# Infini-attention with a gated GLU on one core: warming products, the order of the first norms, the absolute Q in two parts, an engine for the bound rows, and the place of one weight load

## The chip, the cores and the metric

The kernel runs on one core of a Trainium2 chip. The metric is the time of one execution in microseconds. The core has five engines that run their own instruction streams: TensorE (PE in the profile, with its weight loads as PEld), VectorE (DVE), ScalarE (ACT), GpSimd (POOL) and SyncE (SP), which here only issues DMAs. ScalarE also issues a few DMAs. Each stream is executed in its written order.

## What is computed

```python
def _A_ref(x, wq, wk, wv, wo, beta):
...
    phi = lambda t: jnp.where(t > 0, t + 1.0, jnp.exp(t))
    g = _sigmoid(beta).reshape(1, H, 1, 1)
    for s in range(N):
        qs, ks, vs = (q[:, :, s].copy(), k[:, :, s].copy(), v[:, :, s].copy())
        logits = jnp.einsum('bhqd,bhkd->bhqk', qs, ks) * scale + mask
        p = _softmax(logits, axis=-1)
        a_dot = jnp.einsum('bhqk,bhkd->bhqd', p, vs)
        pq = phi(qs)
        num = jnp.einsum('bhld,bhde->bhle', pq, M)
        den = jnp.einsum('bhld,bhd->bhl', pq, z)[..., None] + 1e-06
        a_mem = num / den
        o = g * a_mem + (1.0 - g) * a_dot
        outs.append(o)
        pk = phi(ks)
        M = M + jnp.einsum('bhld,bhle->bhde', pk, vs)
        z = z + jnp.einsum('bhld->bhd', pk)
...
    return o @ wo

def _B_ref(x, w_gate, w_up, w_down):
    g = jnp.einsum('bsd,df->bsf', x, w_gate)
    u = jnp.einsum('bsd,df->bsf', x, w_up)
    h = _sigmoid(g) * u
    return jnp.einsum('bsf,fd->bsd', h, w_down)

x = A_x
xn = _layernorm(x, axis=-1)
s = _A_ref(xn, A_wq, A_wk, A_wv, A_wo, A_beta)
g = _silu(_B_ref(xn, B_w_gate, B_w_up, B_w_down))
return x + s * g
```

In the first function x is the normed input, 2048 x 640; there are 32 heads of 20 and N = 4 segments of L = 512 rows; F is 1536. The result is bfloat16, 2048 x 640.

## The kernel before, in words

The 2048 rows are four segments of 512. A segment's normed input stands transposed in `xnT` (five chunks of 128 channels by 512 rows). From it come K and Q, transposed (`ktd`, `qtd`, five chunks of 128 x 512 each, from `do_K` and `do_Q`), V by rows (`do_V(n, j, half)`: row tile j, 320 columns), and the gate and up products of the GLU (`do_gate`, `do_up`, twelve each a segment).

**Bound.** The softmax subtracts no maximum that is found from the scores. Instead a bound is computed ahead: `do_K` keeps the largest absolute K of each channel (`kabs`), `bound` spreads it over heads (`ik`, line 318) and takes the absolute values of Q (`aq`, line 322, one VectorE instruction over 128 x 2560), and `bound_mm` multiplies the two (five products, line 330) into PSUM tile `cps` of 96 rows. Line 333 copies them to `cb` on VectorE, line 334 writes them to DRAM, and `bound_dma` brings them back as three more rows of each head of `QT`. The tile `aq` shares its one buffer with `odot` (tag `oq`), in which the parts of the memory read-out of a segment are collected and written to DRAM by `mem_spill`.

**Start.** Lines 639 to 703 are written in order by hand. TensorE multiplies zeros (`keep_warm`, 128 x 128 by 128 x 512, into `wps`) until the first tile is there. VectorE makes the statistics of each row tile in two halves (`half_stats0`), ScalarE the root for tiles 0 and 1 (`root0`), GpSimd the power for tiles 2 and 3 (`ln_rstd`), and VectorE the normed tile (`norm0`, line 249). TensorE transposes it, and the transposed tile is copied from PSUM: tile 0 in two parts (`first_transpose`, line 665 on ScalarE, line 663 on VectorE), tiles 1 and 2 on ScalarE (line 266), tile 3 on VectorE (line 268). Between the transposes stand the eight V products. Then follow K and Q of segment 0 (lines 705 to 715), its bound, and the first gate and up products.

**Queue of SP.** After `bound_mm(0)` SP brings back the bound rows of heads 0 to 15, loads the next input (`load_x(1)`, line 141), writes the second part of K and Q (`spill`, line 307), reads K back transposed (`k_tok`, line 374), brings K and Q into the head layout (`relayout`, line 313) with the bound rows of heads 16 to 31, and only then loads `Wd` (line 728, 1920 KB) and `Wo`.

**Body.** From line 734 a planner writes the rest: 20 slots a segment. A slot begins with the scores of one unit (line 541, into the single PSUM tile `Sps`) and their exponential on ScalarE (line 549); between the scores the planner puts dense products and, at the fractions of a slot that `TIMES` lists, the other steps for the next segment m: among them K at 9.75 to 14.4, Q at 11.5 to 13.7, `bound` at 14.8, `bound_mm` at 15.9. A step with a cost of 0 moves no product. All PSUM tiles other than `Sps` come from a pool of four (`ps_d`); a product that needs a new one waits until its last reader is done.

Of the kernel before, what the change touches and what calls it, by code (L numbers as in the profile page):

```python
# [9 lines left out]
P = 128  # L10
# [5 lines left out]
L = 512  # L16
F = 1536
DC = D // P
# [6 lines left out]
BF = mybir.dt.bfloat16  # L25
F32 = mybir.dt.float32
ACT = mybir.ActivationFunctionType
ALU = mybir.AluOpType
# [27 lines left out]
def segment_units(n):  # L56
# [11 lines left out]
    stats0=(0.83, 1.2, 1.95, 3.9), stats=(-0.55, 0.42, 1.32, 3.57), norm=(5.2, 5.75, 6.03, 6.18),  # L68
    norm_T=7.22, ready=12.0, K=(9.75, 10.18, 10.6, 13.9, 14.4), Q=(11.5, 11.9, 12.47, 12.67, 13.7),
    K_eng='vaava', Q_eng='avvav', V=(10.3, 13.3, 14.4, 14.6, 16.35, 17.45, 19.75, 19.85), V_eng='avaavvav',  # L70
    k_spill0=14.77, k_lay0=15.15, q_spill0=14.1, q_lay0=16.33, q_spill1=15.26, k_spill1=17.0, bound=14.8,
    bound_mm=15.9, bound_lay0=18.6, load_x=14.7, phi_k=((7.08, 7.78, 8.23), (12.7, 12.8, 13.7)),
    phi_q=((16.0, 16.6, 17.12), (18.3, 18.7, 19.18)),
)
# [7 lines left out]
def kernel(  # L82
# [14 lines left out]
    nc = tc.nc  # L97
# [160 lines left out]
    def ln_transpose(n, j, xn, eng):  # L258
        if n not in xnT_of:
            xnT_of[n] = xpool.tile([P, DC, L], BF, name="xnT")  # L260
        pT = ps_d.tile([P, DC, P], BF, name="pT", tag="d")
        for c in range(DC):
            nc.tensor.transpose(pT[:, c, :], xn[:, c * P:(c + 1) * P], ident[:])
        dst = xnT_of[n][:, :, j * P:(j + 1) * P]
        if eng is nc.scalar:
            nc.scalar.copy(dst, pT[:])
        else:
            nc.vector.tensor_copy(dst, pT[:])
# [41 lines left out]
    def relayout(n, half, dd, dst, eng):  # L310
        src = dd[n % 2][320 * half:320 * (half + 1), :].rearrange("(g r d) n -> r d g n", g=4, r=4)
        for r in range(4):
            eng.dma_start(dst[32 * r:32 * r + DH, 4 * half:4 * half + 4, :], src[r])

    def bound(n):
        s = seg[n]
        ik = stg.tile([P, DC, H], BF, name="ik")
        nc.vector.tensor_tensor(ik[:], Ind[:].rearrange("p c r g -> p c (r g)"),
                                s["kabs"][:].unsqueeze(2).to_broadcast([P, DC, H]), op=ALU.mult)
        aq = stg.tile([P, DC, L], BF, name="aq", tag="oq")  # L320
        U16 = mybir.dt.uint16
        nc.vector.tensor_scalar(aq[:].bitcast(U16), s["qt"][:].bitcast(U16), 0x7FFF, None, op0=ALU.bitwise_and)
        s["bound"] = ik, aq

    def bound_mm(n):
        ik, aq = seg[n]["bound"]
        cps = ps_d.tile([3 * H, L], F32, name="cps", tag="d")
        for c in range(DC):
            i = c % 3
            nc.tensor.matmul(cps[H * i:H * i + H, :], lhsT=ik[:, c, :], rhs=aq[:, c, :],  # L330
                             start=(c < 3), stop=(c >= 2), tile_position=(0, H * i), skip_group_check=True)
        cb = stg.tile([3 * H, L], BF, name="cb")
        nc.vector.tensor_copy(cb[:], cps[:])  # L333
        nc.sync.dma_start(Bd[n % 2][:], cb[:])

    def bound_dma(n, half):
# [5 lines left out]
    def do_V(n, j, half, evac):  # L342
        ps = ps_d.tile([P, HD], F32, name="psv", tag="d")
        for k in range(DC):
            mm(ps[:], xnT_of[n][:, k, j * P:(j + 1) * P], Wv[:, k, half * HD:(half + 1) * HD],
               k == 0, k == DC - 1)
        dst = V[n % 2][:, j, half * 16:(half + 1) * 16, 0:DH]
        src = ps[:].rearrange("p (h e) -> p h e", e=DH)
        if evac is nc.scalar:
            nc.scalar.copy(dst, src)  # L350
        else:
            nc.vector.tensor_copy(dst, src)
# [282 lines left out]
    def keep_warm(k):  # L635
        for _ in range(k):
            nc.tensor.matmul(wps[:], lhsT=warm[:, 0:P], rhs=warm[:, 0:L], start=True, stop=True)  # L637

    keep_warm(11)
    mv, rs = ln_tiles(0)  # L640
    new_seg(0)
    xns, sts = {}, {}
# [1 line left out]
    def half_stats0(j, i):  # L644
        if i == 0:
            sts[j] = lnp.tile([P, 2, 6], F32, name="st")
        nc.vector.bn_stats(sts[j][:, i, :], xt_of[0][:, j, i * HD:(i + 1) * HD])
        if i == 1:
            nc.vector.bn_aggr(mv[:, j, :], sts[j][:])
# [4 lines left out]
    def first_transpose():  # L654

        xnT_of[0] = xpool.tile([P, DC, L], BF, name="xnT")
        for c0, c1 in ((0, 2), (2, 5)):
            pT = ps_d.tile([P, c1 - c0, P], BF, name="pT", tag="d")
            for c in range(c0, c1):
                nc.tensor.transpose(pT[:, c - c0, :], xns[0][:, c * P:(c + 1) * P], ident[:])  # L660
            dst = xnT_of[0][:, c0:c1, 0:P]
            if c0:
                nc.vector.tensor_copy(dst, pT[:])
            else:
                nc.scalar.copy(dst, pT[:])
# [9 lines left out]
    half_stats0(1, 0)  # L675
    norm0(0)
    half_stats0(1, 1)
    first_transpose()
    root0(1)
    load_w(nc.scalar, Wg, B_w_gate)  # L680
    half_stats0(2, 0)
    norm0(1)
    half_stats0(2, 1)
    ln_rstd(mv, rs, slice(2, 3))
# [1 line left out]
    half_stats0(3, 1)  # L686
    ln_rstd(mv, rs, slice(3, 4))
    norm0(2)
    keep_warm(2)
    do_V(0, 0, 0, nc.scalar)  # L690
    ln_transpose(0, 1, xns[1], nc.scalar)
    norm0(3)
# [3 lines left out]
    do_V(0, 1, 0, nc.scalar)  # L696
    ln_transpose(0, 2, xns[2], nc.scalar)
    do_V(0, 1, 1, nc.scalar)
    do_V(0, 2, 0, nc.scalar)
    ln_transpose(0, 3, xns[3], nc.vector)  # L700
    do_V(0, 2, 1, nc.scalar)
    do_V(0, 3, 0, nc.scalar)
    do_V(0, 3, 1, nc.scalar)
# [4 lines left out]
            spill(0, 0, nc.sync, None)  # L708
    for c in range(3):
        do_Q(0, c, nc.scalar)  # L710
    spill(0, 0, None, nc.sync)
    relayout(0, 0, Kd, KT, nc.sync)
    relayout(0, 0, Qd, QT, nc.sync)
    for c in range(3, 5):
        do_Q(0, c, nc.scalar)
    bound(0)
    finish(do_gate(0, 0))
    finish(do_up(0, 0))
    bound_mm(0)
    bound_dma(0, 0)  # L720
    load_x(1)
    spill(0, 1, nc.sync, nc.sync)
    k_tok(0)
    relayout(0, 1, Kd, KT, nc.sync)
    relayout(0, 1, Qd, QT, nc.sync)
    bound_dma(0, 1)
    gates()
    nc.sync.dma_start(Wd[:], B_w_down.rearrange("(f p) n -> p f n", p=P))
    load_w(nc.sync, Wo, A_wo)
    for f in (1, 2, 3, 4):  # L730
        finish(do_gate(0, f))
# [68 lines left out]
    for n in range(NSEG):  # L800
        t0 = n * SEG

        def on(name, ns, fn, *items):
            times = TIMES[name]
            for i, it in enumerate(items):
                at(t0 + (times[i] if isinstance(times, (list, tuple)) else times), ns, fn, *it)

        if n >= 1:
            on("dot6", 0, dot_spill, (n - 1, 4, 7))
            on("load6", 0, out_load, (n - 1, 0, C4))  # L810
            on("dot7", 0, dot_spill, (n - 1, 7, 8))
            on("load7", 0, out_load, (n - 1, C4, D))
            if n >= 2:
                on("add", 0, out_add, (n - 1, 0, DC - 1), (n - 1, DC - 1, DC))
            on("out", V_NS, out_item, *[(n - 1, i) for i in range(8)])
            on("update", 700, m_update, (n - 1,))
            on("mem", MEM_NS, mem_part, *[(n, i % 4, i // 4) for i in range(8)])
            on("mem_spill", 0, mem_spill, (n,))
            on("mem_T_last" if n == NSEG - 1 else "mem_T", 0, mem_T, (n,))
            if n < NSEG - 1:  # L820
                on("k_tok", 0, k_tok, (n,))
        on("dot3", 0, dot_spill, (n, 0, 4))
        if n == NSEG - 1:
            on("dot5", 0, dot_spill, (n, 4, 6))
            on("load5", 0, out_load, (n, 0, 6 * 4 * DH))
            on("add5", 0, out_add, (n, 0, 3))
            continue
        m = n + 1
        on("stats0" if n == 0 else "stats", 0, stats, *[(m, j) for j in range(4)])
        on("norm", 0, norm, *[(m, j) for j in range(4)])  # L830
        on("norm_T", 0, ln_dmaT, (m,))
        on("ready", 0, ready.add, (m,))
        at(t0 + TIMES["K"][0] - 0.001, 0, new_seg, m)
        on("K", GLU_NS, do_K, *[(m, c, EVAC[TIMES["K_eng"][c]]) for c in range(DC)])
        on("Q", GLU_NS, do_Q, *[(m, c, EVAC[TIMES["Q_eng"][c]]) for c in range(DC)])
        on("V", V_NS, do_V, *[(m, i // 2, i % 2, EVAC[TIMES["V_eng"][i]]) for i in range(8)])
        on("k_spill0", 0, spill, (m, 0, nc.sync, None))
        on("k_lay0", 0, relayout, (m, 0, Kd, KT, nc.sync))
        on("q_spill0", 0, spill, (m, 0, None, nc.sync))
        on("q_lay0", 0, relayout, (m, 0, Qd, QT, nc.sync))  # L840
        on("q_spill1", 0, spill, (m, 1, None, nc.sync))
        on("k_spill1", 0, spill, (m, 1, nc.sync, None))
        on("bound", 0, bound, (m,))
        on("bound_mm", C_NS, bound_mm, (m,))
        on("bound_lay0", 0, bound_dma, (m, 0))
        at(t0 + SEG - 0.003, 0, relayout, m, 1, Kd, KT, nc.sync)
        at(t0 + SEG - 0.002, 0, relayout, m, 1, Qd, QT, nc.sync)
        at(t0 + SEG - 0.001, 0, bound_dma, m, 1)
        for name, sg, key in (("phi_k", n, "ktok"), ("phi_q", m, "qt")):
            for i, (c0, c1) in enumerate(((0, 2), (2, 4 if key == "ktok" else 5))):  # L850
                for fn, t, a in zip((phi_min, phi_exp, phi_end), TIMES[name][i], ((sg, key, c0, c1), (), ())):
                    at(t0 + t, 0, fn, *a)
        if n + 2 < NSEG:
            on("load_x", 0, load_x, (n + 2,))
# [105 lines left out]
```

## Time and profile before

| what | us |
|---|---|
| three runs: median (lowest to highest) | 321.97 (320.97 to 322.71) |
| the profiled execution: its own time | 322.08 |
| the profiled execution: span of its instructions | 320.4 |
| TensorE busy | 310.9 |
| VectorE, ScalarE, GpSimd busy | 230.9, 225.2, 137.4 |
| first warming product, first transpose, first K product begin | 1.24, 5.91, 14.51 |
| first scores begin | 36.83 |
| `bound` of segments 1, 2, 3: `aq` begins | 88.86, 155.84, 222.51 |

All times in the text are from the start of the span. A line of the timeline gives start, duration, engine, line, operation, tiles written and read, and in brackets the idle time before it with what ended it. A product's line reaches past the moment at which the next may start: five products of 320 columns start 0.136 us apart and their group reads 0.84 us.

### The profile page before, as it was taken

What the parts mean: (1) busy time and instruction counts of PE and PEld (TensorE: products, weight loads), DVE (VectorE), ACT (ScalarE), POOL (GpSimd) and SP (SyncE); (2) the same over time, 40 slices, a digit from 0 to 9 for tenths busy, and PEclk for the clock granted to TensorE, in tenths of its full rate; (3) what the DMA queues carried; (4) which work ended last, traced back from release to release, by engine and by line L of the source; (5) the groups of instructions that cost most, each with busy time, mean ns of one, the idle gap of its engine ahead of it and who ended that gap; (6) DMA issues with size and microseconds to landing.
All of it is one profiled execution on the core that took longest, in us unless ns stands there. A gap on an engine that the chain in (4) does not pass through costs nothing.

```text
span 320.4 us, 10046 instructions
## 1 busy us (share of the span) xinstructions
PE 310.9 (97%) x4218; PEld 167.4 (52%) x4247; DVE 230.9 (72%) x503; ACT 225.2 (70%) x225; POOL 137.4 (43%) x231
## 2 busy tenths in 40 slices
PE   8999999999999999999999999999999999999994
PEld 3544434665445445654575445545466645445673
DVE  5384265765779888997778999977877686734555
ACT  3623478788798777777897868778797766776730
POOL 1780035525273445334553364444533353435324
PEclk9999999999999999999999999999999999999999
DMA  7974679320742362606683383436544000350302
GB/s 258 366 308 145 175 165 355 101 49 2 212 149 67 106 156 84 124 23 195 192 188 94 108 127 100 104 119 197 121 133 125 18 23 23 117 133 3 98 19 82
DMA packets 56086, 41.36 MB, mean 129 GB/s; under 512 B 26953, under 2 KB 54665, under 8 KB 56041
## 3 DMA queue, kind: packets, MB, share of 16 engines
q1 hardware_dynamic: 53496, 35.97, 40.5%
q10 hardware_dynamic: 2544, 4.75, 4.0%
q8 instruction: 33, 0.54, 0.7%
q14 instruction: 13, 0.10, 0.1%
HBM read 19.90 MB, written 14.78 MB: 108 GB/s over the span
## 4 chain that ended last, share of the span: by engine, by line
PE 93%; DVE 2%; ACT 2%; issue 1%; POOL 1%; DVEq 0%; ACTq 0%
PE yp L130 11%; PE up L130 11%; PE gp L130 10%; PE psq L130 9%; PE Sps L541 8%; PE gp L134 6%; PE up L134 5%; PE yp L134 5%; PE ApsT L565 5%; PE psv L130 4%; PE psq L134 4%; PE sp L130 3%; PE sp L134 3%; PE sp L527 2%; PE wps L637 2%
## 5 line engine op out<-in xcount | busy, mean ns | idle before, releaser
L549 ACT ACTIVATE pt<-Sps 128x2048 bf16<-128x2048 f32 (+1 forms) x81 | 150.3, 1856 | 42.4 <-PE Sps L541 38.8
L551 POOL TENSOR_SCALAR_AFFINE_SELECT pt<-pt 128x512 bf16<-128x512 bf16 x128 | 82.7, 661 | 158.5 <-ACT pt L549 158.4
L433 DVE SCALAR_TENSOR_TENSOR hT<-tg,up 128x512 bf16<-128x512 bf16 x48 | 32.3, 674 | 22.9 <-PE up L130 8.4
L130 PE MATMUL up<-xnT,Wu 128*128 128x512 bf16 x147 | 40.3, 379 | 1.3 <-issue 1.0
L130 PE MATMUL yp<-Wd,hT 128*128 128x320 bf16 x257 | 40.3, 300 | 0.3 <-issue 0.3
L422 ACT ACTIVATE tg<-gp 128x512 bf16<-128x512 f32 x48 | 28.6, 596 | 16.6 <-PE gp L130 12.6
L130 PE MATMUL gp<-xnT,Wg 128*128 128x512 bf16 x144 | 38.2, 379 | 0.3 <-issue 0.2
L541 PE MATMUL Sps<-QT,KT 23*128 23x128 bf16 (+3 forms) x512 | 32.5, 301 | 0.1
L584 DVE STREAM_TRANSPOSE obT<-ob 128x512 bf16<-128x512 bf16 x30 | 21.1, 704 | 13.4 <-POOL ob L580 13.1
L130 PEld LDWEIGHTS <-hT 128*128 128x128 bf16 x257 | 23.5, 98 | 12.2 <-issue 3.6
L450 DVE SCALAR_TENSOR_TENSOR aa<-t,yp 128x320 bf16<-128x320 bf16 x32 | 15.3, 480 | 12.9 <-ACT t L449 12.8
L134 PE MATMUL gp<-xnT,Wg 128*32 128x512 bf16 x360 | 24.1, 380 | 0.0
L586 DVE STREAM_TRANSPOSE tb<-ApsT 128x512 f32<-128x512 f32 x30 | 21.2, 708 | 2.6 <-PE ApsT L565 2.4
L130 PEld LDWEIGHTS <-Wu 128*128 128x128 bf16 x160 | 14.4, 98 | 16.3 <-issue 3.2
L565 PE MATMUL ApsT<-pt,V 128*32 128x512 bf16 (+2 forms) x480 | 22.8, 299 | 0.0
L541 PEld LDWEIGHTS <-KT 23*128 23x128 bf16 x512 | 9.8, 92 | 24.4 <-issue 24.1
L130 PEld LDWEIGHTS <-Wg 128*128 128x128 bf16 x150 | 14.1, 98 | 16.0 <-issue 1.9
L134 PE MATMUL up<-xnT,Wu 128*32 128x512 bf16 x320 | 21.7, 380 | 0.0
L449 ACT ACTIVATE t<-yp 128x320 bf16<-128x320 f32 x32 | 13.9, 435 | 10.8 <-PE yp L130 9.0
L130 PE MATMUL psv<-Wv,xnT 128*128 128x320 bf16 x130 | 20.8, 299 | 0.4 <-DVE cb L333 0.2
L580 POOL TENSOR_TENSOR ob<-tb,rb 128x320 bf16<-128x320 f32 x27 | 19.8, 732 | 2.3
L134 PE MATMUL yp<-Wd,hT 128*32 128x320 bf16 x508 | 20.2, 300 | 0.0
(122 smaller groups left out, 451.6 us busy)
## 6 DMA issues: line engine op xcount, KB each, us to landing
KT<-Kd SPq DMA_DIRECT2D x32, 80.0 KB
QT<-Qd SPq DMA_DIRECT2D x32, 80.0 KB
out_dram<-xt SPq DMA_DIRECT2D x14, 160.0 KB
Wg<-in_B_w_gate_dram ACTq DMA_DIRECT2D x1, 1920.0 KB
Wu<-in_B_w_up_dram ACTq DMA_DIRECT2D x1, 1920.0 KB
xt<-in_A_x_dram SPq DMA_DIRECT2D x3, 640.0 KB
Wd<-in_B_w_down_dram SPq DMA_DIRECT2D x1, 1920.0 KB
Xd<-xn SPq DMA_DIRECT2D x12, 160.0 KB
```

The source lines that it names most:

```text
L130: nc.tensor.matmul(out_, lhsT=lhsT, rhs=rhs, start=start, stop=stop, skip_group_check=True)
L134: nc.tensor.matmul(out_[cols], lhsT=lhsT[:, cols], rhs=rhs, start=start, stop=stop, tile_position=(0, 32 * r), skip_group_check=True)
L422: nc.scalar.activation(tg[:], gp[:], ACT.Tanh, scale=0.5)
L433: nc.vector.scalar_tensor_tensor(out=h[:], in0=seg[n]["tg"][:], scalar=1.0, in1=up[:], op0=ALU.add, op1=ALU.mult)
L450: nc.vector.scalar_tensor_tensor(out=s["aa"][j][:, hs], in0=t2[:], scalar=1.0, in1=yp[:], op0=ALU.add, op1=ALU.mult)
L541: nc.tensor.matmul(Sps[:, r, c0:c0 + ncol], lhsT=KT[32 * r:32 * r + DH + 3, g, kb * P:(kb + 1) * P], rhs=QT[32 * r:32 * r + DH + 3, g, q0: ...
L549: nc.scalar.activation(pt[:, :, 0:ntot], Sps[:, :, 0:ntot], ACT.Exp, scale=SCALE)
L551: nc.gpsimd.affine_select(out=pt[:, :, c0:c0 + P], in_=pt[:, :, c0:c0 + P], compare_op=ALU.is_ge, fill=0.0, base=0, pattern=[[0, 4], [1, P ...
L565: nc.tensor.matmul(ps[32 * r:32 * r + 32, q0:L], lhsT=Vflat[n % 2][:, off:off + 32], rhs=t[:, r, c0:c0 + ncol], start=(i == 0), stop=(i == ...
L580: nc.gpsimd.tensor_tensor(ob[:, :, 0:DH], tb[:, :, 0:DH], rb[:].unsqueeze(2).to_broadcast([P, L // 32, DH]), op=ALU.mult)
L584: nc.vector.transpose(s["obT", g // 4][:, g % 4, :], ob[:].rearrange("p b e -> p (b e)"))
L586: s["turn", g] = (lambda: nc.vector.transpose(tb[:].rearrange("p b e -> p (b e)"), ps[:]), quotients, turn_back)
```

## The change

There are seven edits.

1. `keep_warm(11)` becomes 9, and the later `keep_warm(2)` becomes 1.
2. The first transposed tile is copied as chunks 0 to 2 on ScalarE and 3 to 4 on VectorE, where it was 0 to 1 and 2 to 4.
3. The first half of the statistics of tile 2 stands ahead of `first_transpose` in VectorE's order, where it stood behind it.
4. The transpose of tile 3 stands ahead of V product (2, 0), where it stood behind it.
5. A new `q_abs` takes the absolute values of Q in two instructions, chunks 0 to 2 and 3 to 4. In segment 0 they stand behind Q 2 and Q 4 and ahead of `ik`; in the body they stand at 13.5 (ahead of Q 4's copy) and at 14.79, behind `bound`, which moves from 14.8 to 14.78 and now makes `ik` alone.
6. `cps` is copied to `cb` by ScalarE.
7. `Wd` is loaded right behind `load_x(1)`, ahead of the second spill of segment 0.

```diff
-    k_spill0=14.77, k_lay0=15.15, q_spill0=14.1, q_lay0=16.33, q_spill1=15.26, k_spill1=17.0, bound=14.8,
+    k_spill0=14.77, k_lay0=15.15, q_spill0=14.1, q_lay0=16.33, q_spill1=15.26, k_spill1=17.0, q_abs=(13.5, 14.79), bound=14.78,
...
+    def q_abs(n, c0, c1):
+        s = seg[n]
+        if c0 == 0:
+            s["aq"] = stg.tile([P, DC, L], BF, name="aq", tag="oq")
+        U16 = mybir.dt.uint16
+        nc.vector.tensor_scalar(s["aq"][:, c0:c1, :].bitcast(U16), s["qt"][:, c0:c1, :].bitcast(U16), 0x7FFF, None,
+                                op0=ALU.bitwise_and)
+
     def bound(n):
...
-        aq = stg.tile([P, DC, L], BF, name="aq", tag="oq")
-        U16 = mybir.dt.uint16
-        nc.vector.tensor_scalar(aq[:].bitcast(U16), s["qt"][:].bitcast(U16), 0x7FFF, None, op0=ALU.bitwise_and)
-        s["bound"] = ik, aq
+        s["bound"] = ik, s["aq"]
...
         cb = stg.tile([3 * H, L], BF, name="cb")
-        nc.vector.tensor_copy(cb[:], cps[:])
+        nc.scalar.copy(cb[:], cps[:])
         nc.sync.dma_start(Bd[n % 2][:], cb[:])
...
-    keep_warm(11)
+    keep_warm(9)
...
-        for c0, c1 in ((0, 2), (2, 5)):
+        for c0, c1 in ((0, 3), (3, 5)):
...
     half_stats0(1, 1)
+    half_stats0(2, 0)
     first_transpose()
     root0(1)
     load_w(nc.scalar, Wg, B_w_gate)
-    half_stats0(2, 0)
     norm0(1)
...
-    keep_warm(2)
+    keep_warm(1)
...
     do_V(0, 1, 1, nc.scalar)
+    ln_transpose(0, 3, xns[3], nc.vector)
     do_V(0, 2, 0, nc.scalar)
-    ln_transpose(0, 3, xns[3], nc.vector)
...
     for c in range(3):
         do_Q(0, c, nc.scalar)
+    q_abs(0, 0, 3)
     spill(0, 0, None, nc.sync)
...
         do_Q(0, c, nc.scalar)
+    q_abs(0, 3, DC)
     bound(0)
...
     load_x(1)
+    nc.sync.dma_start(Wd[:], B_w_down.rearrange("(f p) n -> p f n", p=P))
     spill(0, 1, nc.sync, nc.sync)
...
     gates()
-    nc.sync.dma_start(Wd[:], B_w_down.rearrange("(f p) n -> p f n", p=P))
     load_w(nc.sync, Wo, A_wo)
...
+        on("q_abs", 0, q_abs, (m, 0, 3), (m, 3, DC))
         on("bound", 0, bound, (m,))
```

## The prediction

> **What bounds the kernel now.** First the page's busy shares and the shares of the chain that ended last.
>
> ```profile
> PE 310.9 (97%) x4218; PEld 167.4 (52%) x4247; DVE 230.9 (72%) x503; ACT 225.2 (70%) x225; POOL 137.4 (43%) x231
> ...
> PE 93%; DVE 2%; ACT 2%; issue 1%; POOL 1%; DVEq 0%; ACTq 0%
> ```
>
> TensorE sets the time. What another engine saves counts only where a product waits for it, so I looked for those places: the start, and the bound of the next segment. The chain of waits of the first 16 us:
>
> ```profile
> 1.24 4.88 PE wps L637 x11
> 6.12 0.54 PE pT L660 x5
> 6.68 0.36 DVE xnT L663
> 7.04 0.40 DVE st L647
> 7.44 0.07 DVE rs L669
> ...
> 7.54 0.46 DVE xn L249
> ...
> 8.04 0.47 PE pT L263 x5
> ```
>
> Three things are to be seen. The warming products come right before the first transpose. Behind it the second transpose waits for VectorE, which copies, makes statistics of tile 2 (line 647, on the chain for 0.40) and only then norms tile 1. VectorE's timeline shows the same from its side:
>
> ```profile
> 4.79 0.45 DVE L249 TENSOR_SCALAR xn<-xt,mv,rs 128x640 bf16<-128x640 bf16 x1
> ...
> 5.67 0.21 DVE L649 BATCH_NORM_AGGREGATE mv<-st 128x2 f32<-128x12 f32 x1
> 6.68 0.36 DVE L663 COPY xnT<-pT 128x384 bf16<-128x384 bf16 x1 [0.80 <-PE pT L660]
> ...
> 12.59 0.49 DVE L268 COPY xnT<-pT 128x640 bf16<-128x640 bf16 x1 [1.51 <-PE pT L263]
> ```
>
> Tile 0 is normed at 4.79 + 0.45 = 5.24, but its transpose begins at 5.91; VectorE then idles 0.80. Next the chain around the bound of segment 2, and the waits around that of segment 3:
>
> ```profile
> 154.88 0.70 DVE kabs L295
> ...
> 155.84 0.83 DVE aq L322
> ...
> 156.72 0.34 PE cps L330
> ```
>
> ```profile
> PE psv L130 <- DVE cb L333: 0.2, 1, 0.2
> ```
>
> VectorE holds TensorE there. Last, SP's own timeline:
>
> ```profile
> 32.20 0.40 SPq L141 DMA_DIRECT2D xt<-in_A_x_dram  x1
> ...
> 37.45 2.88 SPq L374 DMA_TRANSPOSE ktok<-Kd  x1
> ...
> 45.85 0.40 SPq L728 DMA_DIRECT2D Wd<-in_B_w_down_dram  x1
> ```
>
> **The start, step by step.** A warming product costs (5.91 - 1.24) / 11 = 0.425. Nine end at 5.06, before tile 0 is there. From a finished norm to the product that waits for it takes 0.05 (tile 1: 7.99 to 8.04). The first transpose begins at 5.24 + 0.05 = 5.29, 0.62 earlier.
>
> ScalarE's copy began 0.46 behind the first transpose (6.37); with a third chunk, 0.11 more (five transposes in 0.53): 5.86. The copy took 0.37 for 256 columns and 0.69 for 640 (line 266), so about 0.48 for 384: it ends at 6.34. The root of tile 1 (0.30) began 0.10 before the copy's end: 6.24 to 6.54. VectorE meanwhile runs the moved statistics from 5.80 (an aggregate is followed 0.13 later, 8.42 to 8.55) to 6.28, and copies two chunks from 6.22 in about 0.29 (0.36 for 384 columns, 0.49 for 640) to 6.51. The reciprocal begins at 6.57, the norm 0.18 later, and it ends at 7.20 instead of 7.99. The moved statistics need tile 2's input: by the trace's packets it had landed by 5.6, so 0.2 is in hand, and each further 0.1 of delay costs 0.1.
>
> The second transpose thus moves from 8.04 to 7.25, 0.79 earlier. Norms, powers and copies of tiles 1 to 3 hang on it in the same order, and move along. The transpose of tile 3 gains more. Before, V (2, 0) waited for ScalarE's copy of tile 2: the products of V (1, 1) ran out at 11.15 and it began at 11.42. The transpose (0.28) then came at 12.11, and V (3, 0) waited another 0.07 for VectorE's copy (12.59 + 0.49). After, tile 3 is normed by 11.09 - 0.79 = 10.30, TensorE is free at 10.36, and the transpose fits the gap of 0.27; the copy ends long before V (3, 0). That saves 0.28 + 0.07 = 0.35. The K products begin at 14.51 - 0.79 - 0.35 = 13.37: **1.14** gained. The one warming product less ahead of the first V product costs and brings nothing: the copy, not it, ends last there (6.34 against 6.25).
>
> The weights must be there earlier too. By the trace's packets Wk had landed by 9.4, Wq by 13.5, Wg by 18.1, Wu by 22.9; they are wanted at 13.4, 18.8, 23.9 and 25.0. The cover is 2.1 for Wu at least. The first scores come at 36.83, and their K, Q and bound rows land by 33.3, 3 us ahead, and move along with the products that feed them.
>
> TensorE's clock is the open term. The page's clock row reads 9 throughout, yet the warming products are 0.425 apart and later products of 512 columns 0.216 (ten of `psq` in 2.32, less 0.17 of tail), so the rate has to be read from the products. It doubled at about 6.5 (five transposes at 0.11, the next two warming products in 0.63 together). After the change TensorE idles 5.06 to 5.29 and 6.25 to 6.39, inside the stretch that was full before. The row gives 6.5 if that does not matter; if it does, every V product until the release takes 5 x 0.267 = 1.33 instead of 0.68. From below: if the rate had doubled at 4.7 in both kernels, the last warming products would have been short, the first transpose not late, and I work out 0.35 gained instead of 1.14. I take 1.0, near the row, since the one profiled execution shows 6.5 and the three runs spread over 1.74 us.
>
> Here a rule bears on it. The Trainium skill, page "TensorE: Matmul & The Clock Gate", section on the clock gate, says that the gate opens after a busy window of about 3.4 us whose place is independent of the kernel, and that what counts is sustained time and not a number of products. That speaks against taking products away: by it the release may fall to the next window, at 6.5 + 3.4 = 9.9, K would begin at 14.5 as before, and the sum would be 321.1 instead of 320.1.
>
> **The bound.** Segment 2: the `yp` products ahead began at 155.18; eight full ones of 0.136 end at 156.27, and `cps` began at 156.72, so 0.45 is lost. After, only chunks 3 and 4 follow `ik`: 1024 columns, for which `phi_min` (same shape and operation, line 361) took 0.40, from 155.84 to 156.24, product at 156.29. Gain 0.43. Then `psv` began at 158.96 though four `yp` from 158.28 ended at 158.82: it waited for `cb`, gain 0.12. Segment 3: `up` at 225.62 was done after 0.22, `psv` began at 226.21 behind `cb` (225.49 + 0.67), gain 0.37. Segment 1: `aq` ended at 89.68 and `cps` began at 89.73 behind products running until 89.70; nothing. Sum **0.92**.
>
> The copy costs ScalarE about 0.59 (its 128x512 casts) four times. Where it lands ScalarE idled: 2.09 before the `tg` at 29.38, 0.56, 1.19 and 0.35 before the exponentials at 91.35, 158.47 and 225.62. Behind the waiting copy stand the next `tg`, for which `hT` waits, and the next exponential, for which the next scores wait. At worst the exponential of segment 1 begins 0.03 later; the next scores (93.66) come 0.4 behind its end. Without that idle, 0.59 each would be on TensorE: 0 to 2.4, I take 0. The first `q_abs` part (1536 columns, about 0.54 between 0.40 for 1024 and 0.82 for 2560) comes ahead of Q 4's copy. It covers itself with VectorE's idle time of 0.77, 0.86 and 0.85 before the last `kabs`. It also waits until `odot` is written out, since it takes its buffer 1.3 slots earlier: landed by 148.3 against about 150 in segment 2, but one packet queue was as late as 217.0 against about 216.7 in segment 3. That uses the last 0.3 of the cover; if it were 0.5 later still, the gain there would be gone: 0 to 0.5, I take 0. No product changes its place in the body, since the new steps have cost 0 and `bound` passes no other step.
>
> **Wd.** SP issues it (0.40) some 14 us earlier. Its 1920 KB take 5.3 at the 366 GB/s of the page's second slice, ahead of the second spill. The read-back (37.45) then starts 5.6 later, the relayouts and bound rows end at about 51.2 instead of 45.62, `Wo` at 52. Behind these stand the normed rows of segment 1: first at 53.79, last at 59.48 by VectorE; then their transpose, landed at 66.0, used at 68.91. All less 1.1; SP has about 0.6 in hand for the first, 5 for the last and 2.9 behind. `ktok` is used at 60.89, the second K and Q at about 70: covered. `Wd` itself landed at 53.6 for a use at 55.03; with TensorE 1.1 earlier only 0.3 would be left, so the move gains nothing and avoids a small stall. I take 0, within 0 and 0.5.
>
> **Sum.** Profiled execution 322.08 (span 320.4 and 1.7 around it) - 1.0 - 0.92 = 320.16; it lay 0.1 above the median of the runs, so 320.1.
>
> **The rivals.** *The clock opens late.* Before, it took 6.5 - 1.24 = 5.3 of unbroken products. If an idle moment starts that count afresh, it opens at 5.29 + 5.3 = 10.6, or, counted from the second idle moment, at 6.39 + 5.3 = 11.7. For it: the idle 0.23 and 0.14. Against: an idle of 0.44 ahead of the transpose at 8.04 came later without harm. At 10.6, V (0, 0) to 7.73, a transpose of 0.53 and V (0, 1) to 9.60 run at half rate and V (1, 0) mostly, to 10.77; two transposes and five V products at full rate (3.96) and 0.1 of waiting for a copy follow: K at 14.83, 0.32 later than before. 322.08 + 0.32 - 0.92 - 0.1 = 321.4; from 11.7 on it is 0.7 late: 321.8.
>
> *Wd in front makes the body wait*; this is the case that ends on the slower side. For it: 1920 KB ahead of a chain of small transfers, each of which waits for the one before. Against: the cover above. If SP ends that chain at F, the last normed rows leave 1.1 later, and `xnT` is there 6.5 after that (59.48 to 66.0) for a use at 67.8: it waits from F = 60.2 on, 14 late instead of 5.6, and every us more costs one. `Wd` at the page's mean rate of 129 GB/s would take 15 and make SP 15.3 late: 321.3. From 16 late on the change is slower than before; at 18 it is 324.0.
>
> *The bound does not get faster*, because VectorE with the early part is late elsewhere, or `odot` lands late: 321.0.
>
> **How the numbers follow.** Forecast 0.70 (319.3 to 320.9: the start's gain between 0.35 and 1.14, the bound's with or without the 0.5 of `odot`, and some 0.5 of the runs' own spread); clock 0.14; Wd 0.08; bound 0.08. A measurement of this kernel can tell about 0.5% (1.6 us) from no change, so 320.36 and 323.6 divide. Of the forecast 0.54 lies below the first and 0.16 above, of the bound's rival 0.02 below, of Wd's 0.06 above the second. Faster 0.56, same 0.38, slower 0.06. The range 319.3 to 322.0 leaves out Wd's 0.08, 0.06 below and a little of the clock's above.
>
> **What would show it.** The first transpose near 5.3, the second near 7.25, K near 13.4, the transpose of tile 3 before V (2, 0); products of 512 columns at 0.216 from 6.5 on (or later: the clock); `cps` of segment 2 without a wait for `aq`, no `psv` waiting for `cb`; exponentials no later against their scores; SP's `Wo` at about 51. The forecast is wrong if V products stand 0.267 apart, if VectorE waits for tile 2's input or for `odot`'s write, or if the first K of segment 1 waits for `xnT`.

## The result, and the profile after

The changed kernel takes 320.23 us (median of 11 runs, 319.72 to 321.94), the kernel before 321.93 (11 runs, 320.97 to 322.71). The ratio is 0.9954, 95% interval 0.9937 to 0.9971: 1.5 us or 0.46% faster by the ratio, 1.7 us by the medians. 320.1 was forecast. The profiled execution has a span of 318.2 instead of 320.4.

The page of the changed kernel, the same two lines:

```profile
PE 312.3 (98%) x4244; PEld 167.1 (53%) x4244; DVE 229.3 (72%) x503; ACT 227.2 (71%) x229; POOL 136.6 (43%) x231
...
PE 97%; ACT 1%; DVE 1%; issue 0%; ACTq 0%
```

TensorE's share of the chain that ended last rose from 93 to 97%: what went is waiting, and of work three warming products. The chain of waits of the first 16 us after (start, duration, engine, tile, line):

```profile
1.24 4.02 PE wps L642 x9
...
5.28 0.51 PE pT L665 x3
...
5.82 0.49 ACT xnT L670
...
6.35 0.87 PE psv L130 x5
...
7.25 0.47 PE pT L263 x5
...
10.51 0.28 PE pT L263 x5
10.79 2.72 PE psv L130 x20
```

The first transpose begins at 5.28 (5.29 was worked out), the second at 7.25 (7.25), and the transpose of tile 3 stands before the last four V products, which now run without a wait. The first K weight load is at 13.21 instead of 14.38. VectorE's timeline shows where its part went:

```profile
5.95 0.49 DVE L652 BATCH_NORM_STATS2 st<-xt 128x6 f32<-128x320 bf16 x1
6.36 0.28 DVE L668 COPY xnT<-pT 128x256 bf16<-128x256 bf16 x1
...
6.74 0.45 DVE L249 TENSOR_SCALAR xn<-xt,mv,rs 128x640 bf16<-128x640 bf16 x1
```

The statistics of tile 2 fill the time that VectorE idled. They began at 5.95 and not at 5.80: in this execution tile 2's input landed at 5.93 instead of 5.59. That cost nothing: ScalarE's root was done at 6.49 and the reciprocal began at 6.55, where 6.57 was worked out. The chain around the bound of segment 2:

```profile
154.22 1.20 PE yp L134 x32
155.42 0.20 PE cps L335
155.62 0.32 PE ApsT L570 x2
```

Neither `kabs` nor `aq` is on it any more. SP's timeline:

```profile
31.98 0.51 SPq L729 DMA_DIRECT2D Wd<-in_B_w_down_dram  x1
...
41.73 2.79 SPq L379 DMA_TRANSPOSE ktok<-Kd  x1
...
49.87 0.40 SPq L144 DMA_DIRECT2D Wo<-in_A_wo_dram  x1
```

I lined up the products of the two traces and followed how much earlier each begins. They are 1.16 earlier from the first K product on, 0.99 behind slot 6, then 1.44 behind `cps` and 1.6 behind `psv` of segment 2, 1.83 from 169 on, and 2.13 behind the `psv` of segment 3. The start and the bound gave 1.16 and 0.89 (0.45, 0.13, 0.31). Two further steps, -0.17 at slot 6 and +0.24 at 169, were in no term of the sum.

### The profile page after: what moved, and what is told of

It is laid out like the page before. It is cut to its first block, busy times and chain, and to the rows that moved or that the text cites. A ratio compares the mean times of both kernels' runs of the same rounds, so it can differ in the third digit from the quotient of the medians.

```text
span 318.2 us, 10079 instructions
## 1 busy us (share of the span) xinstructions
PE 312.3 (98%) x4244; PEld 167.1 (53%) x4244; DVE 229.3 (72%) x503; ACT 227.2 (71%) x229; POOL 136.6 (43%) x231
## 3 DMA queue, kind: packets, MB, share of 16 engines
HBM read 19.90 MB, written 14.78 MB: 109 GB/s over the span
## 4 chain that ended last, share of the span: by engine, by line
PE 97%; ACT 1%; DVE 1%; issue 0%; ACTq 0%
PE up L130 11%; PE yp L130 11%; PE gp L130 10%; PE psq L130 10%; PE Sps L546 9%; PE gp L134 6%; PE up L134 6%; PE yp L134 6%; PE psv L130 6%; PE ApsT L570 5%; PE psq L134 4%; PE sp L130 3%; PE sp L134 3%; PE sp L532 2%; PE psv L134 1%; PE wps L642 1%
## 5 line engine op out<-in xcount | busy, mean ns | idle before, releaser
L130 PE MATMUL up<-xnT,Wu 128*128 128x512 bf16 x160 | 43.0, 380 | 0.0
L130 PE MATMUL gp<-xnT,Wg 128*128 128x512 bf16 x150 | 39.3, 380 | 0.0
L454 ACT ACTIVATE t<-yp 128x320 bf16<-128x320 f32 x32 | 13.9, 435 | 10.4 <-PE yp L130 8.7
```

The lines of the kernel that those rows point to most:

```text
L130: nc.tensor.matmul(out_, lhsT=lhsT, rhs=rhs, start=start, stop=stop, skip_group_check=True)
```

## The experiments

Ratios are to the kernel before, run beside each, with 95% intervals.

**The start alone.**

```diff
-    keep_warm(11)
+    keep_warm(9)
-        for c0, c1 in ((0, 2), (2, 5)):
+        for c0, c1 in ((0, 3), (3, 5)):
+    half_stats0(2, 0)
     first_transpose()
...
-    half_stats0(2, 0)
     norm0(1)
-    keep_warm(2)
+    keep_warm(1)
+    ln_transpose(0, 3, xns[3], nc.vector)
     do_V(0, 2, 0, nc.scalar)
-    ln_transpose(0, 3, xns[3], nc.vector)
```

> Only the edits of the start (9 and 1 warming products, three chunks on ScalarE, the statistics of tile 2 early, the transpose of tile 3 early); the bound and Wd as before. Theory (the parts add up): first K product at 13.35 instead of 14.51, all later products earlier by the same 1.1 to 1.2; in segments 2 and 3 the waits for aq and cb (0.45, 0.12, 0.37) are still there; time 1.0 below before, about 320.9. Rival (the start's gain came from a full clock that by chance opened at 5.85 instead of 6.51): the first K product moves by less than 0.7 when the rate doubles at 6.5 or later. Second rival (given back later): K at 13.35, but the first scores not 1.1 earlier.

Ratio 0.9982 (0.9966 to 0.9998): 0.6 us faster, with an interval from 0.1 to 1.1: below the 1.0 expected, which the interval still holds. In the trace the step is there in full. The first K weight load is at 13.18 with a clock that opened at 6.20, and the first scores are at 35.64 instead of 36.83. So neither rival holds: it is not the early clock, and nothing is given back before the scores. The waits at the bound are still there, as this chain of segment 2 shows:

```profile
154.66 0.83 DVE aq L322
...
155.53 0.34 PE cps L330
```

One wait was new: V product (0, 1) waited 0.3 for the second half of Wv. It is wanted at 7.5 instead of 8.3, and the prediction, which went through the covers of Wk, Wq, Wg and Wu, left Wv out.

**The bound alone.**

```diff
+        on("q_abs", 0, q_abs, (m, 0, 3), (m, 3, DC))
         on("bound", 0, bound, (m,))
...
-        nc.vector.tensor_copy(cb[:], cps[:])
+        nc.scalar.copy(cb[:], cps[:])
```

(with the new `q_abs` and its calls in segment 0)

> Only the absolute Q in two parts and the copy of the bound rows on ScalarE; the start and Wd as before. Theory: K at 14.5 as before; cps of segment 2 does not wait for aq, psv of segments 2 and 3 does not wait for cb; the products after the bound of segment 2 are 0.55, those after that of segment 3 0.9 earlier; time 0.9 below before, 321.0. Rival (most of the gain is the start's, the bound's waits are refilled by other waits of VectorE or ScalarE): under 0.3 in all, 321.6 or more.

Ratio 0.9998 (0.9982 to 1.0014): no gain at all. Yet no product waits for `aq` or `cb`: behind the bound of segment 2 the products are 0.46 earlier, having been 0.12 to 0.16 late since slot 6. Then 0.68 is lost at one place. TensorE's weight loads there, and the list of its products' waits:

```profile
167.94 0.39 PEld L130 LDWEIGHTS <-hT 128*128 128x128 bf16 x4 [0.21 <-issue]
169.64 0.10 PEld L130 LDWEIGHTS <-hT 128*128 128x128 bf16 x1 [1.32 <-issue]
```

```profile
PE yp L130 <- issue: 1.0, 1, 1.0
```

TensorE stands between two products of one group that wait for no data. "Issue" means that nothing the profile follows holds it. The two products begin at 168.36 and 169.65, 1.29 apart where the others are 0.136 apart; the excess, 1.15, is called the gap from here on. In the kernel before it was 0.47 at the same place:

```profile
168.39 0.39 PEld L130 LDWEIGHTS <-hT 128*128 128x128 bf16 x4 [0.21 <-issue]
169.41 0.10 PEld L130 LDWEIGHTS <-hT 128*128 128x128 bf16 x1 [0.64 <-issue]
```

The DMA packets give a hint. Queue 8, which the page names "instruction", brings 16 KB 33 times in an execution, one packet for some 257 of TensorE's 8500 instructions. One of these packets began at 167.10 and was through at 168.26; TensorE went on 1.38 later. In the kernel before, the packet was through at 168.05, and TensorE went on 1.37 later. What filled the DMA engines just ahead is seen in the windows of this run (columns: window, its length, busy time of PE, PEld, DVE, ACT and POOL with instructions, clock, DMA share, GB/s; the DMA share counts the packets that begin in a window and can pass 1):

```profile
166.00:167.00 1.00, 1.00 (x40) 0.91 (x32) 0.96 (x3) 0.70 (x3) 0.74 (x1) 1.00 1.28 290
167.00:168.00 1.00, 1.00 (x29) 0.50 (x22) 0.96 (x5) 1.00 (x1) 0.00 (x0) 1.00 1.00 302
168.00:169.00 1.00, 0.66 (x5) 0.24 (x4) 0.97 (x3) 0.94 (x2) 0.00 (x0) 1.00 0.20 58
169.00:170.00 1.00, 0.35 (x3) 0.28 (x4) 1.00 (x2) 1.00 (x1) 0.00 (x0) 1.00 0.02 8
```

The engines are full until about 168, up to 167.37 with `oTm`, the transposed read-back of the memory part: 640 KB in packets of 256 bytes, issued by SP at 161.66 and taking 4.14 to issue. That made a new theory: the fetch of TensorE's next instructions stands behind these packets, and the gap swallows what the bound gives.

**Wd alone, and the change without it.**

```diff
     load_x(1)
+    nc.sync.dma_start(Wd[:], B_w_down.rearrange("(f p) n -> p f n", p=P))
...
-    nc.sync.dma_start(Wd[:], B_w_down.rearrange("(f p) n -> p f n", p=P))
```

> Only Wd moved ahead of the second spill; the rest as before. Theory: no product moves, time within 0.2 of before, 321.9; the read-back of K is issued 4 to 6 us later. Rival (it gains because Wd was late): first yp product and all behind it earlier by 0.2 to 0.5. Rival on the other side (the exponential of slot 6, 0.33 late in the changed kernel at 57.4, was late because of Wd's place): it is late here too, and the scores behind it by 0.17.

Ratio 0.9999 (0.9984 to 1.0013). The trace's first K weight load is at 13.92, 0.46 earlier, but Wd comes after it; this run's clock opened at 5.59 instead of 6.51, and that moved it. Behind the start no product gains on the others before 168, and the exponential of slot 6 is not late.

> The changed kernel with Wd back in its old place behind the bound rows of heads 16 to 31. Theory (Wd has cover in both places): no yp product waits for it, or for 0.3 at most; 320.2 to 320.5. Rival (the parts do not add because Wd is late once TensorE is 1.1 earlier): the first yp waits 0.5 or more, 320.8 or above.

Ratio 0.9953 (0.9935 to 0.9971), the changed kernel's own. The first `yp` follows `up` without a wait:

```profile
52.87 1.05 PE L134 MATMUL up<-xnT,Wu 128*32 128x512 bf16 x16
53.74 2.21 PE L134 MATMUL yp<-Wd,hT 128*32 128x320 bf16 x60
```

Wd's move neither gains nor costs measurably.

**Warming products alone** (9 and 1, the rest as before).

> Only 9 and 1 warming products instead of 11 and 2. Theory: the first transpose begins at 5.29 (0.62 earlier), the copies behind it move by as much, VectorE's statistics of tile 2 follow its copy as before; second transpose at 7.42, K at 13.9; time 0.6 below before, 321.3. Rival (the products were needed for the clock): the rate doubles at 9 or later, V products stand 0.267 apart, K at 14.4 or later and no gain.

Ratio 0.9988 (0.9974 to 1.0001), 0.4 us, not clear of zero. The first transpose is at 5.22, the second at 7.54 and the first K weight load at 13.87, a product 0.13 later, so 14.0 against the 13.9 expected. The products were not needed for the clock in this execution; it opened at 4.46.

**Four warming products in the changed kernel.**

```diff
-    keep_warm(9)
+    keep_warm(4)
```

> The changed kernel with 4 warming products at the start instead of 9. Theory (the clock opens after some 3.4 of steady work, and 0.2 of idle does not count against it but 2.3 does): TensorE idles from 2.95 to 5.29, the rate doubles between 8.7 and 12.1, the V products until then stand 0.267 apart, K begins at 14.2 to 15.3 instead of 13.35; time 1 to 2 above the changed kernel, 321.2 to 322.2. Rival (the clock opens at a set time whatever TensorE does): the rate doubles at 7.5 or earlier and K begins by 13.7.

Ratio 0.9970 (0.9955 to 0.9985), 0.5 us above the changed kernel's, whose interval overlaps this one; 1 to 2 was expected. In the trace the clock opened at 10.99 and the first K weight load is at 14.82, as expected. TensorE's timeline shows V products at half rate until then, five taking 1.51 where later ones take 0.84:

```profile
1.24 1.89 PE L642 MATMUL wps<-mn 128*128 128x512 bf16 x4 [1.24 <-DVE mn L155]
5.33 0.72 PE L665 MATMUL pT<-ident,xn 128*128 128x128 bf16 x5 [2.20 <-DVE xn L249]
...
6.40 1.51 PE L130 MATMUL psv<-Wv,xnT 128*128 128x320 bf16 x5
...
11.23 0.84 PE L130 MATMUL psv<-Wv,xnT 128*128 128x320 bf16 x5
```

So with an idle of 2.2 the clock opened later than in any other trace (4.2 to 7.3); the 0.2 that the change leaves did not send it back.

**ScalarE's copy made twice** in the changed kernel.

```diff
         nc.scalar.copy(cb[:], cps[:])
+        nc.scalar.copy(cb[:], cps[:])
```

> The changed kernel with ScalarE's copy of the bound rows made twice (0.59 more, four times); the result is the same. Theory (the copy stands in ScalarE's idle time): the second copy uses up the idle 0.56, 1.19 and 0.35 of the three segments and more: the exponential behind it late by 0.6 at most in segments 1 and 3, TensorE late by under 0.4 in all; 320.2 to 320.6. Rival (ScalarE sets the pace there): every copy shows on TensorE, 0.59 x 3 = 1.8 later, 322.0.

Ratio 0.9973 (0.9958 to 0.9987), 0.6 us above the changed kernel's, with intervals that overlap: more than the theory's 0.4, far from the rival's 1.8. ScalarE in segment 2:

```profile
156.01 0.59 ACT L338 CAST cb<-cps 96x512 bf16<-96x512 f32 x1
156.64 0.58 ACT L339 CAST cb<-cps 96x512 bf16<-96x512 f32 x1
157.12 1.88 ACT L555 ACTIVATE pt<-Sps 128x2048 bf16<-128x2048 f32 x1
```

The products behind the bounds of segments 2 and 3 lose 0.1 and 0.2. The gap at 167.5 is 0.7 larger than in the changed kernel's trace (0.89 and 0.23), and 0.2 goes near 269, which I can't assign. One copy in ScalarE's idle time is nearly free.

**The read-back later.**

```diff
-    update=-1.6, mem=(2.1, 3.8, 3.0, 6.1, 7.0, 2.3, 9.0, 10.0), mem_spill=11.56, mem_T=16.8,
+    update=-1.6, mem=(2.1, 3.8, 3.0, 6.1, 7.0, 2.3, 9.0, 10.0), mem_spill=11.56, mem_T=17.7,
```

> The bound's two edits alone (as in the run before), and besides the transposed read-back of the memory part (oTm, 640 KB in packets of 256 bytes) issued at slot 17.7 of each segment instead of 16.8, 3 us later. Theory (TensorE ran out of instructions at 168.5 for 1.15 us, because the fetch of its next 16 KB stood behind that read-back's packets on the DMA engines): the gap of 1.3 before the next weight load is gone or under 0.3, the products behind it stand 0.7 earlier than in the run without this edit; time 0.6 to 0.9 below that run, 321.0. Rival (the gap comes from the place of TensorE's program alone): a gap of 0.4 or more at the same product, time 321.7.

> The changed kernel with the same later read-back (slot 17.7). Theory of the fetch: its gap of 0.23 at 167.5 goes, nothing else moves: 0.0 to 0.3 below the changed kernel, 320.0. Rival (the read-back now lands in the way of another fetch, or holds SP ahead of the bound rows): a new gap, 320.3 or more.

Both went the wrong way: 1.0023 (1.0004 to 1.0042) with the bound's edits, 0.9993 (0.9969 to 1.0017) with the whole change. The expectation had the timing wrong. SP runs behind the slots there, so the later place only put one more spill ahead: in the second run `oTm` was issued at 161.44, 1.0 later than in the changed kernel, not 3. That sets its packets more squarely in the fetch's way. The instruction packets now began at 167.87 and 167.21, and the gaps are 2.0 and 2.2. The windows of the second run show what follows (PEclk is the column with 0.50):

```profile
166.00:170.00 4.00, 1.96 (x32) 1.12 (x25) 3.91 (x11) 2.83 (x2) 1.05 (x2) 1.00 0.67 168
170.30:173.60 3.30, 3.30 (x28) 1.50 (x29) 1.40 (x3) 1.60 (x3) 0.92 (x2) 0.50 0.44 138
174.00:178.00 4.00, 3.84 (x83) 2.10 (x77) 2.20 (x6) 2.33 (x4) 0.63 (x1) 1.00 0.33 71
```

TensorE idled for 2 us, and its clock closed to half for 3.41 us. Behind it the products of this execution are 3.4 later than the changed kernel's. In the first run's trace the clock closed in the same way. Both profiled executions are among the slowest of their runs (324.43 and 323.37, where the medians are 322.44 and 321.05), so most executions can't have lost as much.

**The read-back earlier.**

```diff
-    update=-1.6, mem=(2.1, 3.8, 3.0, 6.1, 7.0, 2.3, 9.0, 10.0), mem_spill=11.56, mem_T=16.8,
+    update=-1.6, mem=(2.1, 3.8, 3.0, 6.1, 7.0, 2.3, 9.0, 10.0), mem_spill=11.56, mem_T=16.0,
```

> The bound's two edits alone, with oTm at slot 16.0. Theory of the fetch: the gap of 1.3 near 168.5 is gone, and the bound's 0.8 to 0.9 shows in full: 0.9 below the kernel before with the same early oTm, 0.9 to 1.3 below the kernel before, 320.5 to 320.9. Rival (the bound's edits gain nothing alone, whatever the fetch): 321.3 or more.

> The kernel before with oTm at slot 16.0 and nothing else. Theory of the fetch: its gap of 0.47 at 168.8 goes, the waits at the bound stay: 0.2 to 0.5 below the kernel before, 321.1 to 321.4. Rival: no difference.

> The changed kernel with the transposed read-back of the memory part (oTm) earlier in SP's order: slot 16.0, ahead of the relayout of Q, instead of 16.8. Theory (TensorE's next 16 KB of instructions wait at the DMA engines until the packets of oTm are through, and TensorE stands until 1.38 after they have come): the packets of oTm are through 1.5 or more earlier, so is the fetch, and the gap at the products of 167.5 (0.23 to 0.95 in the runs so far) is gone; 0.2 to 0.6 below the changed kernel, 319.7 to 320.0. Rival (the fetch is late for another reason): the gap is 0.2 or more, time as the changed kernel's, 320.2. Second rival (Q's relayout comes too late for the scores of slot 20): scores near 169 wait.

With the bound's edits: 0.9968 (0.9951 to 0.9984), where they gave nothing without this line. `oTm` is issued at 159.29, and at the same product nothing is left of the gap, for which the weight loads stood 1.32:

```profile
167.88 0.56 PEld L130 LDWEIGHTS <-hT 128*128 128x128 bf16 x5 [0.21 <-issue]
168.44 1.32 PEld L130 LDWEIGHTS <-xnT 128*128 128x128 bf16 x10
```

The kernel before with the line alone: 0.9994 (0.9980 to 1.0007); its gap is 0.24 instead of 0.47, and its time has not measurably changed. Between these two the bound's edits are worth 0.9 (medians 320.92 and 321.84), as forecast, or 0.8 by the ratios, whose intervals just overlap. The changed kernel with the line: 0.9942 (0.9924 to 0.9959), median 320.25. Its interval overlaps the changed kernel's, so it isn't told apart from it. The trace shows why little can be left: its gap of 0.23 at 167.5 is gone, but the second rival came. The four scores that follow take twice as long as the changed kernel's (first line: the changed kernel):

```profile
169.30 0.42 PE L546 MATMUL Sps<-QT,KT 23*128 23x512 bf16 x4
...
169.24 0.84 PE L546 MATMUL Sps<-QT,KT 23*128 23x512 bf16 x4
```

What they waited for the trace does not name; the relayout of Q was issued 4.1 later than in the changed kernel and the bound rows behind it 2.3 later. In the run with the bound's edits the four scores from 170.16 on begin over 0.27, where the changed kernel's begin over 0.05.

The large gaps are thus settled by moving their cause both ways: the gap grew to 2.0 and 2.2 with the packets later, and was 0, 0 and 0.24 with them earlier. The start of the instruction packet says the same: in eight of the fourteen traces it lies 0.2 to 0.3 before the end of the read-back's last packet, and all gaps over 0.5 are among these; in the other six it lies 0.0 to 1.7 behind that end, and the gap is 0.47 at most. The small gap has another part: with the line alone the read-back was through at 165.10 and the instruction packet still began only at 166.78, and 0.24 is left. The size of the gap is not fixed in one program, either. Without Wd's move it was 1.08 in a body that is otherwise the changed kernel's, whose own was 0.23. How large it is on average, and so what share of the lost 0.9 it explains in the medians, one profile a kernel can't say.

## Why the prediction was right, and where not

- **The start** was worked out at 1.14 and taken as 1.0; the two profiled executions show 1.16, and each step stands within 0.1 of its forecast time but the moved statistics and the copy behind them (5.95 for 5.80, 6.36 for 6.22; both hidden).
- **The clock** was rightly the open term. The table has every profiled execution. In the old order the opening matters: the first K weight load is at 13.9 for 5.59, at 14.38 from 6.5 on. In the new order it is at 13.07 to 13.21 whatever the opening, but for one run in which tile 0 was normed 0.3 late. So, by the table, the start is worth 0.7 to 1.3 according to where the opening falls. This is the mechanism of the lower end, 0.35 at an opening of 4.7, which no run reached.

| warming products | clock opens at | first K weight load |
|---|---|---|
| 11 and 2, old order | 5.59; 6.12; 6.51; 6.55; 7.17; 7.26 | 13.92; 14.18; 14.38; 14.37; 14.37; 14.38 |
| 9 and 1, old order | 4.46 | 13.87 |
| 9 and 1, new order | 4.18; 4.38; 5.09; 5.85; 6.20; 6.44 | 13.07; 13.38; 13.09; 13.21; 13.18; 13.17 |
| 4 and 1, new order | 10.99 | 14.82 |

- **The rival of the late clock** did not come, but its working was sound: it put the first K product at 14.83 for an opening at 10.6, and with four warming products that product began at 14.96 for 10.99. Its count of 5.3 from the last idle moment was wrong for an idle of 0.2.
- **The rule of the Trainium skill** (page "TensorE: Matmul & The Clock Gate", section on the clock gate) says that the window is about 3.4 us long and placed independently of the kernel. These runs agree: full clock lasted 163.84, half clock 3.413, a 48th of it, in both runs with the gap of 2 us, and the openings with 9 or 11 products spread over 4.2 to 7.3. What the prediction drew from it against taking products away holds at four, not at nine.
- **The bound**: 0.92 forecast, 0.89 in the trace, and 0.9 between two kernels with the early read-back.
- **Wd** and **ScalarE's copy**: taken as 0. Wd is 0 both ways; the copy costs at most about 0.3 in all, judged by what a second one cost at the bounds (0.1 and 0.2).
- **Two signs of being wrong** that the prediction named did come, and cost nothing. VectorE waited for tile 2's input until 5.95, as told above; the prediction had every 0.1 beyond 5.8 cost 0.1. And in segment 3 it waited 0.43 for the write of `odot`, as the line below shows. Its idle time before the last `kabs` took that up (0.24 of it were left), and the bound of segment 3 still gained 0.31 of its 0.37.

```profile
215.34 0.56 DVE L320 TENSOR_SCALAR aq<-qtd 128x1536 uint16<-128x1536 uint16 x1 [0.43 <-DMA Od<-odot]
```

- **What the sum left out.** The 1.92 that it adds up lies inside the measured 0.9 to 2.0, so the total held. But it took TensorE as waiting at the start and the bound alone. The profile before also had TensorE's gap of 0.47 between 168.81 and 169.42, with "issue" as its releaser, and no step of the prediction spoke of it. How large such a gap gets depends, as the runs with the moved read-back show, on when that transfer meets a fetch, so it can grow when the body moves. So the bound's term did not stand by itself: alone it gave 0.0 (-0.5 to 0.6) instead of 0.92, the start alone 0.6, both together 1.5. That the total came so near is partly luck: in the two profiles the steps left out, -0.17 and +0.24, nearly cancel. The dividing line of 0.5% lies inside the measured interval (0.29 to 0.63%), so on which side of it the change falls is not decided.
- **Left open**: 0.17 lost at slot 6, where the exponential began 0.33 late without a wait that the profile names. It shows in the changed kernel and in all three runs with the bound's edits alone, not with Wd alone nor with the copy made twice.

## What to carry to other kernels

When one engine runs without a break, look at its "issue" gaps too: here the packet with the next instructions came only as a large transfer in small packets ran out. A gain that is seen step by step in the trace but not in the time may have gone to such a place, as the bound's did; try moving the transfer, and look at what then comes later. Warming products need only reach the first real product closely enough: here nine did, eleven held it up, and four left a hole of 2.2 us, behind which products ran at half the clock until 10.99.

## What was not expected of the hardware

- Instructions arrive in 16 KB packets on a queue of their own, 33 in an execution; by their number and by the gaps they are TensorE's. In the ten traces with a gap at 167 to 170 it went on 1.17 to 1.52 us after such a packet was through, in eight of them 1.36 to 1.46.
- 640 KB in 256-byte packets kept the DMA engines full for about 3 us (a DMA share of 1.06 to 1.28 in the windows from 164 to 167, with the bound alone), and the instruction packet, at 167.10, began only as they ran out.
- A gap of 2.0 to 2.2 us on TensorE was enough for its clock to close to half for 3.41 us; gaps of up to 1.15 never did.
